# A Fourier layer, an RWKV channel mix and a Mish layer in one kernel: the first transform step with native fp32 operands for every piece

## Chip, cores and metric

The kernel runs on one core of one Trainium2 chip. The metric is the device time of one execution in microseconds, lower is better; of several runs the median is given. Every tensor is fp32 outside the kernel, and the outputs have to agree with the reference to fp32-like accuracy: this is why most operands of TensorE stand in two halves of a reduced type (fp32r), a high half `h` and a low half `l`, and most products are three matmuls (high by high, high by low, low by high).

## What is computed

With 4 sequences of 3072 rows and 256 columns, the reference is, cut to what matters:

```
X  = rfft(x, axis=1)                         # over the 3072 rows
Yr = Xr @ w_r - Xi @ w_i + b_r ; Yi = Xr @ w_i + Xi @ w_r + b_i
Y  = soft threshold of Yr and Yi by 0.01
y  = irfft(Y)                                # back to 3072 rows
xk, xr = mixes of y with y shifted by one row
r * ((relu(xk @ w_k) ** 2) @ w_v)            # r = sigmoid(xr @ w_r)
h  = that @ w_in ; out = (h * tanh(softplus(h))) @ w_out
```

## The kernel before

**The Fourier transform** is done in two steps of matmuls. Row number n is written as 32 n1 + n2, with n1 below 96 and n2 below 32. *Step one* (`s1`) multiplies, for each n2, the 96 x 256 matrix of x by a 96 x 96 matrix of cosines and sines. It goes by pieces of four n2: 8 pieces for each of the 4 sequences, 32 in all, numbered i = 8b + q. A piece is loaded into a tile `xs` (96 x 1024), its four products come into two PSUM tiles `s1p`, are copied out by `s1_ev` (two copies of 96 x 512), and are stored to DRAM. *Step two* (`s2`) reads them back in 48 units u of two groups of rows (tile `A`), 12 units for a sequence. For each unit the kernel then mixes with w_r and w_i (`mix`), adds the two parts (`yt`), applies the threshold (`above`, `shrink`, in the course of which GpSimd moves halves of the tile Y), and does the first inverse step (`is1`), whose result is stored to DRAM. The *last inverse step* (`is2`, its results copied out by `is2_ev`) belongs to the next stage, which goes by 32 tiles of 384 rows, but for the first two tiles it is done early, between the last units (`early`).

**Two forms of step one.** The first 12 pieces (`NAT = 12`) use x and the matrix as they are, in fp32: one matmul instruction of the program for each product. For the 20 others, x is split by `split_x` into `xh` (ScalarE, line 77) and `xl` (VectorE, line 78), the matrix has been split into FC by `split_F`, and each product is three matmuls (line 333).

**The order of work** is the order of the code. No scheduler moves anything: each engine has one queue, which it follows in order, and the buffers of a tile pool (`bufs=`) are reused in turn. DMAs are issued by SyncE (SP), also in order. An iteration of the transform loop, number u, issues `s2(u+1)`; the copies of `is1(u-3)`; the copies and stores of the last piece; the split of the s2 result into `Xh` (ScalarE) and `Xl` (VectorE); up to two steps of a background queue (`bg`), which loads and decodes the weights of the next stage on VectorE; a load and a split of `A`; `mix(u)`; the split of `Y(u-1)`; `above` and `shrink` of unit u; if the iteration is in `S1_AT`, a piece of step one with the load of piece i + 3 and the split of piece i + 2; `is1(u-2)`; two more background steps. The PSUM tile of `s2` has one buffer, so `s2(u+2)` on TensorE waits for `Xl` of unit u+1. Iterations 2 to 5 and two of each three from 8 to 30 hold a piece.

At the end of the loop, at u = 48 and 49, `early(14)` and `early(15)` do the last inverse step of the second tile, four products of each of its halves at a time.

The functions that the change touches and what calls them:

Of the kernel before, what the change touches and what calls it, by code (L numbers as in the profile page):

```python
# [8 lines left out]
F32 = mybir.dt.float32  # L9
F32R = mybir.dt.float32r  # L10
# [7 lines left out]
B, S, D, FK, FF = 4, 3072, 256, 1024, 2048  # L18
N1, N2 = 96, 32
NG = 12  # L20
NU = B * NG
# [8 lines left out]
def kernel(  # L30
# [27 lines left out]
    nc = tc.nc  # L58
# [13 lines left out]
    def split(src, hi, lo, lo_eng=None, hi_eng=None):  # L72

        if hi_eng is nc.vector:
            nc.vector.tensor_copy(out=hi, in_=src)
        else:
            nc.scalar.copy(out=hi, in_=src)  # L77
        (lo_eng or nc.vector).tensor_tensor(out=lo, in0=src, in1=hi, op=ALU.subtract)  # L78
# [66 lines left out]
    pkp = pk.__enter__()  # L145
# [5 lines left out]
    XS0 = [pkp.tile([128, 4, 4, D], F32, tag=w, name="XS0", bufs=1) for w in ("WK", "WV")]  # L151
# [4 lines left out]
    p1p = p1.__enter__()  # L156
    p1s = tc.tile_pool(name="p1s", bufs=1, side="left", reuse_waits="tile")
    p1sp = p1s.__enter__()
    ps1 = tc.tile_pool(name="ps1", bufs=2, space=PSUM, reuse_waits="tile")
    ps1p = ps1.__enter__()  # L160

    FC = p1sp.tile([128, N2, 2, N1], F32R, name="FC")
    MC = p1p.tile([128, 2, 2, 192], F32R, name="MC")
    WC = p1p.tile([128, 2, 2, 128], F32R, name="WC")
    WX = p1p.tile([128, 2, 3, 2, D], F32R, name="WX")
# [1 line left out]
    SEL = p1p.tile([128, 2, 128], F32R, name="SEL")  # L167
    ZV = p1p.tile([128, 2, 2, 128], F32R, name="ZV")

    Ft = {}  # L170

    def new_F(q):
        tag, n = ((("dec_v", 1), ("dec_b", 1)) + (("Cs", 2),) * 2 + (("A", 4),) * 4)[q]
        Ft[q] = p1p.tile([128, 512], F32, tag=tag, name="ctmp", bufs=n)

    def load_F(q):
        for c in (slice(0, 192), slice(192, 384)) if q == 0 else (slice(0, 384),):
            nc.sync.dma_start(out=Ft[q][0:N1, c], in_=c_f[:, q * 384 + c.start:q * 384 + c.stop])
            yield

    def split_F(q):
        v = Ft[q][0:N1, 0:384].rearrange("p (n c) -> p n c", n=4)
        split(v, FC[0:N1, 4 * q:4 * q + 4, 0, :], FC[0:N1, 4 * q:4 * q + 4, 1, :])

    cst = {}

# [90 lines left out]
    xs_t, xh_t, s1_t = {}, {}, deque()  # L277

    def new_x(b, q):
        t = xs_t[b, q] = p1sp.tile([128, 4, D], F32, tag="xs", name="xs", bufs=3) if b else XS0[q // 4][:, q % 4]  # L280

    def x_loads(b, q):
        xv = x[b].rearrange("(p n) d -> p n d", n=N2)[:, 4 * q:4 * q + 4, :]
# [6 lines left out]
        for _ in x_loads(b, q):  # L290
            pass

    def split_x(b, q):
        t = xs_t.pop((b, q))
        h = p1sp.tile([128, 4, D], F32R, tag="xh", name="xh", bufs=3)
        l = p1sp.tile([128, 4, D], F32R, tag="xl", name="xl", bufs=3)
        split(t[0:N1], h[0:N1], l[0:N1])
        xh_t[b, q] = (h, l)

    def warm(n):  # L300
        z = p1p.tile([128, 512], F32, tag="yt", name="zero", bufs=1)
        nc.vector.memset(z[:, 0:256], 0.0)
        p = ps1p.tile([128, 2, 512], F32, tag="s2", name="warm", bufs=1)
        for _ in range(n):
            nc.tensor.matmul(out=p[:, 0, 0:256], lhsT=z[:, 0:128], rhs=z[:, 0:256], start=True, stop=True)

    NAT = 12

    def s1(b, q):
        i = 8 * b + q  # L310
        plain = i < NAT
        if plain:
            h = xs_t.pop((b, q))
            f = Ft[q][:, 0:384].rearrange("p (n c) -> p n c", n=4)
        else:
            h, l = xh_t.pop((b, q))
        if b == 0:
            st = XS0[q // 4][0:N1, q % 4]
        elif i < 11:
            st = pkp.tile([N1, 4, D], F32, tag=("D", "Dh", "Dl")[q], name="st", bufs=1)  # L320
        else:
            st = p1sp.tile([N1, 4, D], F32, tag="st", name="st", bufs=2)
        for e in range(2):
            p = ps1p.tile([N1, 2, D], F32, tag=("s1" if i >= NAT or e == 0 else "mx"), name="s1p")
            for m in range(2):
                n2 = 4 * q + 2 * e + m
                if plain:
                    nc.tensor.matmul(  # L328
                        out=p[:, m, :], lhsT=f[0:N1, 2 * e + m, :], rhs=h[0:N1, 2 * e + m, :], start=True, stop=True
                    )  # L330
                    continue
                for k, (w, v) in enumerate(((0, h), (0, l), (1, h))):
                    nc.tensor.matmul(
                        out=p[:, m, :], lhsT=FC[0:N1, n2, w, :], rhs=v[0:N1, 2 * e + m, :],
                        start=(k == 0), stop=(k == 2),
                    )
            s1_t.append((b, q, e, st, p))

    def s1_ev():
        b, q, e, st, p = s1_t.popleft()  # L340
        if e == 1 or 8 * b + q >= NAT:
            nc.scalar.copy(out=st[:, 2 * e:2 * e + 2, :], in_=p)
        else:
            nc.vector.tensor_copy(out=st[:, 0:2, :], in_=p)
        if e == 1 and b == 0:
            nc.sync.dma_start(out=scr1a[:, 4 * q:4 * q + 4, :], in_=st[0:32])
            if q < 4:
                store_rest(q)
        elif e == 1 and 8 * b + q >= 11:
            nc.sync.dma_start(out=scr1[b][:, 4 * q:4 * q + 4, :], in_=st)  # L350
        elif e == 1:
            kept[q] = st
# [6 lines left out]
    def store_rest(q):  # L359
        nc.sync.dma_start(out=scr1[0][32:N1, 4 * q:4 * q + 4, :], in_=XS0[q // 4][32:N1, q % 4])  # L360
# [57 lines left out]
    def mix(u):  # L418
        hl = Xh.pop(u)
        last = u % NG == GS  # L420
        p = ps1p.tile([128, 2, D], F32, tag="mx", name="mxp")
        k1 = ps1p.tile([128, D], F32, tag="k1", name="k1p", bufs=1)

        def terms(c, w):
            return [
                (hl[a][:, dh, 128 * c:128 * c + 128], WX[:, dh, w, b, :])
                for dh in range(2) for (a, b) in ((0, 0), (0, 1), (1, 0))
            ]

        def put(out, ts, start, stop=True):  # L430
            for i, (a, w) in enumerate(ts):
                nc.tensor.matmul(out=out, lhsT=a, rhs=w, start=(start and i == 0), stop=(stop and i == len(ts) - 1))  # L432

        put(k1, terms(2, 0), True)
        nc.tensor.matmul(out=p, lhsT=SEL[:, int(last), :], rhs=BR, start=True, stop=False)
        put(p[:, 0, :], terms(1, 2), False, False)
        ts = terms(0, 1)
        if last:
            ts += [(ZV[:, a, dh, :], WX[:, dh, 0, b, :]) for dh in range(2) for (a, b) in ((0, 0), (0, 1), (1, 0))]
        put(p[:, 1, :], ts, False)  # L440
        ks = p1p.tile([128, D], F32, tag="K1", name="K1", bufs=1)
        nc.scalar.copy(out=ks, in_=k1)
        t = p1p.tile([128, 2, D], F32, tag="yt", name="yt", bufs=1)
        nc.vector.tensor_tensor(out=t, in0=p, in1=ks.unsqueeze(1).to_broadcast([128, 2, D]), op=ALU.add)  # L444
        mx_t[u] = t
# [153 lines left out]

    warm(3)  # L600
    for q in range(8):
        new_F(q)
        new_x(0, q)
    def load_both(q):
        for _ in zip(load_F(q), x_loads(0, q)):
# [3 lines left out]
        load_both(q)  # L609
    for q in range(8):  # L610
        s1(0, q)
        split_F(q)
        s1_ev()
        s1_ev()
        if q < 3:
            load_both(q + 5)
        elif q == 3:
            load_consts()
            load_x(1, 0)
        elif q == 4:  # L620
            load_x(1, 1)
# [39 lines left out]
    split_A(2)  # L661
    load_A(4)
    split_W()
    split_x(1, 4)
    split_A(3)

    WK = pkp.tile([128, 2, 2, FK], F32R, tag="WK", name="WK", bufs=1)
# [59 lines left out]
    U_E = 32  # L727
    for u in range(NU + 3):
        if 0 < u < NU - 1:
            s2(u + 1)  # L730
        if u > 2:
            is1_ev(u - 3)
        if s1_t:
            s1_ev()

        def fill():
            while s1_t:
                s1_ev()
            if u > 2:
                bg(2)  # L740

        if 0 < u < NU - 1:
            s2_ev(u + 1, fill)
        else:
            fill()
        if u + 5 < NU:
            load_A(u + 5)
        if 0 < u < NU - 3:
            split_A(u + 3)
        if u < NU:  # L750
            mix(u)
        if 1 <= u <= NU:
            split_Y(u - 1)
        if u < NU:
            above(u)
            shrink(u)
        if u == 0:
            load_x(1, 6)
            split_x(1, 5)
        if u in S1_AT:  # L760
            i = 8 + S1_AT[u]
            s1(*divmod(i, 8))
            if i + 3 < 8 * B:
                load_x(*divmod(i + 3, 8))
            if i + 2 < 8 * B:
                split_x(*divmod(i + 2, 8))
        if NU <= u < NU + 2:
            early(u - U_E - 2)
        if 2 <= u < NU + 2:
            is1(u - 2)  # L770
        if u > 2:
            bg(2)
        if u == U_E:
            p1s.__exit__(None, None, None)
            pEg = tc.tile_pool(name="pE", bufs=1, side="left", reuse_waits="tile")
            pE[0] = pEg.__enter__()
        if U_E < u < NU - 1:
            early(u - U_E - 1)
# [425 lines left out]
    for P in range(2, 8 * NBLK + LAG):  # L1204
        t, q = divmod(P, 8)
# [111 lines left out]
```

## Time and profile before

| | |
|---|---|
| median of 3 runs | 1999.83 us (1996.97 to 2003.06) |
| the profiled execution | 2000.01 us, span 1998.0 us |
| TensorE (PE) busy | 1966.9 us, 98% |
| weight loads (PEld) busy | 1867.9 us, 93% |
| VectorE (DVE) busy | 1517.6 us, 76% |
| ScalarE (ACT) busy | 1172.5 us, 59% |
| GpSimd (POOL) busy | 121.9 us, 6% |

The shares are means over three stages: the transforms (to about 320 us), the channel mix (to about 1000 us) and the Mish layer. Engine names: PE is TensorE's matmuls, PEld its weight loads, which overlap them, DVE VectorE, ACT ScalarE, POOL GpSimd, SP the queue that issues DMAs. L333 is line 333 of the kernel. Each row of a timeline has start, duration, engine, line, operation, the tiles written and read, and in brackets how long the engine had been idle and what ended that. A matmul's end is modelled and holds its way through the array, so matmuls in a row overlap; the pitch between their starts is what they cost. A native fp32 matmul of the program shows as two MATMUL records, each with its weight load.

### The profile page before, as it was taken

What the parts mean: (1) busy time and instruction counts of PE and PEld (TensorE: products, weight loads), DVE (VectorE), ACT (ScalarE), POOL (GpSimd) and SP (SyncE); (2) the same over time, 40 slices, a digit from 0 to 9 for tenths busy, and PEclk for the clock granted to TensorE, in tenths of its full rate; (3) what the DMA queues carried; (4) which work ended last, traced back from release to release, by engine and by line L of the source; (5) the groups of instructions that cost most, each with busy time, mean ns of one, the idle gap of its engine ahead of it and who ended that gap; (6) DMA issues with size and microseconds to landing.
All of it is one profiled execution on the core that took longest, in us unless ns stands there. A gap on an engine that the chain in (4) does not pass through costs nothing.

```text
span 1998.0 us, 33277 instructions
## 1 busy us (share of the span) xinstructions
PE 1966.9 (98%) x13026; PEld 1867.9 (93%) x13026; DVE 1517.6 (76%) x2441; ACT 1172.5 (59%) x1793; POOL 121.9 (6%) x196
## 2 busy tenths in 40 slices
PE   8999999999999999999999999999999999999999
PEld 6988888999999999999999999999999999999998
DVE  5889897677777777776587778777787877787785
ACT  4777777777777777776544444444444444444444
POOL 1333331000000000000000000000000000000000
PEclk9999999999999999999999999999999999999999
DMA  9666532112121121211101001001000010000000
GB/s 289 182 192 198 170 110 84 60 51 78 49 68 61 57 70 51 68 49 42 41 22 32 22 24 30 22 22 33 22 29 25 22 32 22 23 31 22 22 12 22
DMA packets 71745, 123.04 MB, mean 62 GB/s; under 512 B 6370, under 2 KB 48580, under 8 KB 71588
## 3 DMA queue, kind: packets, MB, share of 16 engines
q1 hardware_dynamic: 68004, 108.33, 18.2%
q0 software_dynamic: 3584, 12.58, 1.6%
q8 instruction: 103, 1.69, 0.4%
q14 instruction: 54, 0.44, 0.1%
HBM read 70.56 MB, written 50.33 MB: 61 GB/s over the span
## 4 chain that ended last, share of the span: by engine, by line
PE 89%; DVE 5%; ACT 3%; issue 2%; DMA 1%; POOL 0%; SPq 0%; DVEq 0%; ACTq 0%; POOLq 0%
PE h L1133 20%; PE o L1181 18%; PE kp L879 14%; PE vp L917 13%; PE o L1182 9%; PE pp L856 3%; PE p L1133 3%; PE pp L556 3%; PE s2p L389 1%; DVE Xl L78 1%; PE mxp L432 1%; PE s1p L328 1%; DVE yt L444 1%; PE hp L822 1%; ACT xh L77 1%
## 5 line engine op out<-in xcount | busy, mean ns | idle before, releaser
L1181 PE MATMUL o<-WO,gh 128*128 128x512 f32 x1536 | 562.0, 394 | 0.0
L1182 PE MATMUL o<-WO,gl 128*128 128x256 f32 x1536 | 430.3, 280 | 0.0
L1133 PE MATMUL h<-xS,WS 128*128 128x256 f32 x2208 | 350.9, 281 | 0.0
L1146 ACT COPY p1s<-p 128x256 f32<-128x256 f32 x184 | 68.5, 372 | 472.0 <-PE p L1133 471.0
L1181 PEld LDWEIGHTS o<-WO,gh 128*128 128x128 f32 x1536 | 288.9, 188 | 43.3
L1133 PEld LDWEIGHTS h<-xS,WS 128*128 128x128 f32 x2208 | 299.6, 188 | 16.1
L879 PE MATMUL kp<-xk,WK 128*128 128x384 f32 x1536 | 291.0, 337 | 0.0
L1182 PEld LDWEIGHTS o<-WO,gl 128*128 128x128 f32 x1536 | 289.5, 188 | 0.2
L917 PE MATMUL vp<-kh,WV 128*128 128x384 f32 x1024 | 281.3, 336 | 0.0
L879 PEld LDWEIGHTS kp<-xk,WK 128*128 128x128 f32 x1536 | 267.6, 189 | 0.3
L1136 DVE TENSOR_TENSOR C<-h,p1s 128x512 f32<-128x512 f32 x184 | 126.9, 690 | 157.7 <-PE h L1133 154.8
L904 DVE TENSOR_TENSOR kl<-kr,kh 128x768 fp32r<-128x768 f32 x128 | 122.8, 959 | 161.4 <-ACT kr L903 161.2
L1118 DVE TENSOR_TENSOR gl<-g,gh 128x1024 fp32r<-128x1024 f32 x184 | 223.4, 1214 | 2.1 <-ACT g L1115 2.1
L1114 ACT ACTIVATE gh<-C 128x1024 fp32r<-128x1024 f32 x184 | 195.7, 1064 | 10.6 <-DVE C L1136 10.5
L1115 ACT ACTIVATE g<-C 128x1024 f32<-128x1024 f32 x184 | 193.1, 1049 | 0.0
L1133 PE MATMUL h<-xS,WI 128*128 128x256 f32 x1104 | 189.8, 280 | 0.0
L1136 DVE TENSOR_TENSOR C<-h,wu 128x512 f32<-128x512 f32 x368 | 187.2, 550 | 0.3 <-PE h L1133 0.3
L917 PEld LDWEIGHTS vp<-kh,WV 128*128 128x128 f32 x1024 | 186.3, 188 | 0.0
L917 PE MATMUL vp<-kl,WV 128*128 128x384 f32 x512 | 171.5, 335 | 0.0
L902 ACT ACTIVATE kh<-kr 128x768 fp32r<-128x768 f32 x128 | 108.3, 846 | 89.1 <-PE vp L917 89.0
L1133 PEld LDWEIGHTS h<-xS,WI 128*128 128x128 f32 x1104 | 155.7, 188 | 0.0
L1136 DVE TENSOR_TENSOR wu<-h,C 128x512 f32<-128x512 f32 x184 | 126.4, 687 | 35.7 <-PE h L1133 31.8
(189 smaller groups left out, 3166.3 us busy)
## 6 DMA issues: line engine op xcount, KB each, us to landing
scr<-Cs SPq DMA_DIRECT2D x48, 256.0 KB
D<-scr SPq DMA_DIRECT2D x32, 384.0 KB
x2d<-r POOLq DMA_DIRECT2D x32, 384.0 KB, 3.5
x<-x2d SPq DMA_DIRECT2D x24, 512.0 KB
out_dram<-ob SPq DMA_DIRECT2D x96, 128.0 KB
A<-scr SPq DMA_DIRECT2D x44, 256.0 KB
xs<-in_x_dram SPq DMA_DIRECT2D x24, 384.0 KB
scr<-st SPq DMA_DIRECT2D x24, 384.0 KB
```

Source lines behind the costliest of these rows:

```text
L879: nc.tensor.matmul(out=p[:, m, 0:TA], lhsT=WK[:, dh, w, f * 128:(f + 1) * 128], rhs=hl[:, v, dh, :], start=(i == 0), stop=(i == 5),)
L902: nc.scalar.activation(out=kh, in_=kr, func=AF.Square)
L904: nc.vector.tensor_tensor(out=kl, in0=kr, in1=kh, op=ALU.subtract)
L917: nc.tensor.matmul(out=p[:, o, 0:TA], lhsT=WV[:, f, w, o * 128:(o + 1) * 128], rhs=v[:, m, :], start=(f == 0 and i == 0), stop=(f == 7 and ...
L1114: nc.scalar.activation(out=gh, in_=c, func=AF.Mish)
L1115: nc.scalar.activation(out=g, in_=c, func=AF.Mish)
L1118: nc.vector.tensor_tensor(out=gl, in0=g, in1=gh, op=ALU.subtract)
L1133: nc.tensor.matmul(out=out, lhsT=a(l), rhs=xS[:, v, b, :], start=(n == 0), stop=(n == 2))
L1136: nc.vector.tensor_tensor(out=out, in0=x0, in1=x1, op=ALU.add)
L1146: nc.scalar.copy(out=p1s, in_=p1)
L1181: nc.tensor.matmul(out=o[m], lhsT=gh[:, m2, ms], rhs=WO[:, f], start=(f == 0), stop=False)
L1182: nc.tensor.matmul(out=o[m][:, 0, :], lhsT=gl[:, m2, ms], rhs=WO[:, f, 0, :], start=False, stop=(f == 15))
```

## The change

All 32 pieces of step one take the native form. FC holds the unsplit fp32 matrix and is loaded directly; `split_F` and `split_x` go, and with them the tiles `xh`, `xl` and `st`. The results of a piece are copied over its own x, in `xs`, which gets seven buffers in place of three. Apart from that, in the last two iterations the early inverse steps are issued ahead of the split of Y instead of behind the pieces.

```
-    FC = p1sp.tile([128, N2, 2, N1], F32R, name="FC")
+    FC = p1sp.tile([N1, N2, N1], F32, name="FC")
...
-    def split_F(q):
-        v = Ft[q][0:N1, 0:384].rearrange("p (n c) -> p n c", n=4)
-        split(v, FC[0:N1, 4 * q:4 * q + 4, 0, :], FC[0:N1, 4 * q:4 * q + 4, 1, :])
...
-        t = xs_t[b, q] = p1sp.tile([128, 4, D], F32, tag="xs", name="xs", bufs=3) if b else XS0[q // 4][:, q % 4]
+        t = xs_t[b, q] = p1sp.tile([128, 4, D], F32, tag="xs", name="xs", bufs=7) if b else XS0[q // 4][:, q % 4]
...
-    def split_x(b, q):
-        t = xs_t.pop((b, q))
-        h = p1sp.tile([128, 4, D], F32R, tag="xh", name="xh", bufs=3)
-        l = p1sp.tile([128, 4, D], F32R, tag="xl", name="xl", bufs=3)
-        split(t[0:N1], h[0:N1], l[0:N1])
-        xh_t[b, q] = (h, l)
...
     def s1(b, q):
...
+        x_ = xs_t.pop((b, q))[0:N1]
         for e in range(2):
-            p = ps1p.tile([N1, 2, D], F32, tag=("s1" if i >= NAT or e == 0 else "mx"), name="s1p")
+            p = ps1p.tile([N1, 2, D], F32, tag=("s1" if 8 * b + q >= 12 or e == 0 else "mx"), name="s1p")
             for m in range(2):
...
-                for k, (w, v) in enumerate(((0, h), (0, l), (1, h))):
-                    nc.tensor.matmul(
-                        out=p[:, m, :], lhsT=FC[0:N1, n2, w, :], rhs=v[0:N1, 2 * e + m, :],
-                        start=(k == 0), stop=(k == 2),
-                    )
-            s1_t.append((b, q, e, st, p))
+                nc.tensor.matmul(
+                    out=p[:, m, :], lhsT=FC[:, 4 * q + 2 * e + m, :], rhs=x_[:, 2 * e + m, :], start=True, stop=True
+                )
+            s1_t.append((b, q, e, x_, p))
...
     split_W()
-    split_x(1, 4)
     split_A(3)
...
         if u < NU:
             mix(u)
+        if NU <= u < NU + 2:
+            early(u - U_E - 2)
         if 1 <= u <= NU:
             split_Y(u - 1)
...
         if u == 0:
             load_x(1, 6)
-            split_x(1, 5)
         if u in S1_AT:
             i = 8 + S1_AT[u]
             s1(*divmod(i, 8))
             if i + 3 < 8 * B:
                 load_x(*divmod(i + 3, 8))
-            if i + 2 < 8 * B:
-                split_x(*divmod(i + 2, 8))
-        if NU <= u < NU + 2:
-            early(u - U_E - 2)
         if 2 <= u < NU + 2:
             is1(u - 2)
```

On VectorE, in the middle of the transform loop, an iteration with a piece stood like this between two Xl (dec_v and dec_b are decode steps of the weights, Al, yt, Yl and Y belong to the units):

```order
L78 TENSOR_TENSOR Xl<-s2p,Xh 128x768
L78 TENSOR_TENSOR Al<-A,Ah 128x512
L444 TENSOR_TENSOR yt<-mxp,K_1165 128x512
L78 TENSOR_TENSOR Yl<-Y,Yh 128x512
L455 SCALAR_TENSOR_TENSOR Y<-yt,yc 128x512
L78 TENSOR_TENSOR xl<-xs,xh 96x1024
L118 TENSOR_SCALAR dec_v<-dec_raw 128x512
L78 TENSOR_TENSOR Xl<-s2p,Xh 128x768
```

and the same place with the change:

```order
L78 TENSOR_TENSOR Xl<-s2p,Xh 128x768
L78 TENSOR_TENSOR Al<-A,Ah 128x512
L406 TENSOR_TENSOR yt<-mxp,K_1064 128x512
L78 TENSOR_TENSOR Yl<-Y,Yh 128x512
L417 SCALAR_TENSOR_TENSOR Y<-yt,yc 128x512
L118 TENSOR_SCALAR dec_v<-dec_raw 128x512
L78 TENSOR_TENSOR Xl<-s2p,Xh 128x768
```

Only xl has gone from the queue between the two Xl; ScalarE loses the cast xh in the same way, and TensorE's twelve matmuls of line 333 become four instructions of line 296.

On ScalarE, at the end of the loop (u = 48 to 50), the rows from the last but one Yh on stood like this (yT and ya are the copies of the early inverse steps, Cs those of `is1`):

```order
L77 CAST Yh<-Y 128x512
L449 ACTIVATE yc<-yt 128x512
L486 COPY Cs<-i1p 128x512
L77 CAST Yh<-Y 128x512
L566 COPY yT<-yT 128x3x32 x2
L569 COPY ya<-s1p 128x192
L566 COPY yT<-yT 128x3x32 x2
L569 COPY ya<-s1p 128x192
L486 COPY Cs<-i1p 128x512
L569 COPY ya<-s1p 128x192 x2
L486 COPY Cs<-i1p 128x512
```

and with the change:

```order
L77 CAST Yh<-Y 128x512
L411 ACTIVATE yc<-yt 128x512
L448 COPY Cs<-i1p 128x512
L528 COPY yT<-yT 128x3x32 x2
L531 COPY ya<-s1p 128x192
L528 COPY yT<-yT 128x3x32 x2
L531 COPY ya<-s1p 128x192
L77 CAST Yh<-Y 128x512
L448 COPY Cs<-i1p 128x512
L531 COPY ya<-s1p 128x192 x2
L448 COPY Cs<-i1p 128x512
```

The last Yh has moved from ahead of the first two pairs of yT and ya to behind them; TensorE's own order there is unchanged, and SP issues the same transfers in the same order.

## Rows read from the trace of the kernel before

**Rows 1.** Windows (span, busy us of PE, PEld, DVE, ACT, POOL; clock, DMA).

```profile
15.00:20.00 5.00, 5.00 (x25) 3.76 (x24) 3.27 (x6) 2.79 (x7) 0.00 (x0) 1.00 1.05 352
35.00:40.00 5.00, 3.45 (x17) 2.88 (x18) 4.46 (x6) 2.37 (x5) 3.73 (x5) 0.79 1.03 310
51.03:230.75 179.72, 170.23 (x1286) 160.93 (x1287) 159.91 (x224) 136.32 (x257) 57.98 (x91) 0.98 0.62 185
230.75:310.76 80.01, 74.67 (x562) 69.31 (x561) 74.18 (x121) 56.13 (x112) 26.94 (x47) 1.00 0.42 127
320.00:600.00 280.00, 280.00 (x1684) 280.00 (x1683) 201.30 (x333) 206.11 (x297) 9.04 (x13) 1.00 0.21 63
```

**Rows 2.** Chain that ended last: starts of step two in undisturbed iterations.

```profile
58.70 1.32 PE s2p L389 x12
...
64.55 1.33 PE s2p L389 x12
...
173.17 1.32 PE s2p L389 x12
...
177.60 1.32 PE s2p L389 x12
```

**Rows 3.** Waits of PE from 51 to 231 us: total, times, longest.

```profile
PE s2p L389 <- DVE Xl L78: 9.6, 8, 2.2
PE s1p L333 <- ACT st L342: 1.3, 3, 0.8
```

**Rows 4.** The chain ahead of the longest wait.

```profile
154.71 1.04 ACT xh L77
...
155.77 1.36 DVE xl L78
...
158.74 0.88 DVE Xl L78
...
159.66 1.50 PE s2p L389 x10
```

**Rows 5.** Native pieces before: timeline of PE, then line 328's durations (ns, min/median/max).

```profile
19.76 1.67 PE L328 MATMUL s1p<-XS,ctmp 96*96 96x256 f32 x7
22.15 1.94 PE L328 MATMUL s1p<-XS,ctmp 96*96 96x256 f32 x8 [0.71 <-DMA XS<-in_x_dram]
...
38.06 3.48 PE L328 MATMUL s1p<-xs,ctmp 96*96 96x256 f32 x8
...
L328 PE MATMUL s1p<-XS,ctmp x64: 379/379/713, 3.9 to 23.7; 96*96 96x256 f32 x64
```

**Rows 6.** Groups by line, 51.03 to 230.75 us: the splits of x.

```profile
L78 DVE TENSOR_TENSOR xl<-xs,xh 96x1024 fp32r<-96x1024 f32 x18 | 24.4, 1358 | 4.4 <-ACT xh L77 4.4
L77 ACT CAST xh<-xs 96x1024 fp32r<-96x1024 f32 x18 | 18.6, 1033 | 0.0
```

**Rows 7.** Timeline of ACT, DVE and PE at the loop's start.

```profile
47.69 1.03 ACT L77 CAST xh<-xs 96x1024 fp32r<-96x1024 f32 x1
...
48.75 1.36 DVE L78 TENSOR_TENSOR xl<-xs,xh 96x1024 fp32r<-96x1024 f32 x1 [0.25 <-ACT xh L77]
50.04 0.94 DVE L78 TENSOR_TENSOR Xl<-s2p,Xh 128x768 fp32r<-128x768 f32 x1
...
51.03 0.47 PE L389 MATMUL s2p<-MC,Ah 128*128 128x192 f32 x2 [2.13 <-DVE Xl L78]
```

**Rows 8.** Timeline of ACT, DVE and PE at the loop's end.

```profile
314.91 0.62 ACT L77 CAST Yh<-Y 128x512 fp32r<-128x512 f32 x1 [1.80 <-POOL Y L459]
...
315.56 0.69 DVE L78 TENSOR_TENSOR Yl<-Y,Yh 128x512 fp32r<-128x512 f32 x1 [2.12 <-ACT Yh L77]
...
316.79 0.33 PE L556 MATMUL s1p<-ifh,Dh 96*128 96x192 f32 x1 [2.66 <-ACT ya L569]
```

**Rows 9.** Chain that ended last: the first matmuls of the next stage, later ones.

```profile
319.39 5.03 PE kp L879 x24
...
326.50 2.08 PE kp L879 x12
```

More of the change, by code (lines that the diff above doesn't have):

```diff
@@ L168 @@
     ZV = p1p.tile([128, 2, 2, 128], F32R, name="ZV")
[L170 to L174, printed above, removed]
     def load_F(q):
+        v = FC[:, 4 * q:4 * q + 4, :].rearrange("p n c -> p (n c)")
         for c in (slice(0, 192), slice(192, 384)) if q == 0 else (slice(0, 384),):
-            nc.sync.dma_start(out=Ft[q][0:N1, c], in_=c_f[:, q * 384 + c.start:q * 384 + c.stop])
+            nc.sync.dma_start(out=v[:, c], in_=c_f[:, q * 384 + c.start:q * 384 + c.stop])
             yield
-    def split_F(q):
-        v = Ft[q][0:N1, 0:384].rearrange("p (n c) -> p n c", n=4)
-        split(v, FC[0:N1, 4 * q:4 * q + 4, 0, :], FC[0:N1, 4 * q:4 * q + 4, 1, :])
     cst = {}
@@ L305, in warm @@
             nc.tensor.matmul(out=p[:, 0, 0:256], lhsT=z[:, 0:128], rhs=z[:, 0:256], start=True, stop=True)
-    NAT = 12
     def s1(b, q):
[L310 to L322, printed above, removed]
+        x_ = xs_t.pop((b, q))[0:N1]
         for e in range(2):
-            p = ps1p.tile([N1, 2, D], F32, tag=("s1" if i >= NAT or e == 0 else "mx"), name="s1p")
+            p = ps1p.tile([N1, 2, D], F32, tag=("s1" if 8 * b + q >= 12 or e == 0 else "mx"), name="s1p")
             for m in range(2):
-                n2 = 4 * q + 2 * e + m
-                if plain:
-                    nc.tensor.matmul(
-                        out=p[:, m, :], lhsT=f[0:N1, 2 * e + m, :], rhs=h[0:N1, 2 * e + m, :], start=True, stop=True
-                    )
-                    continue
-                for k, (w, v) in enumerate(((0, h), (0, l), (1, h))):
-                    nc.tensor.matmul(
-                        out=p[:, m, :], lhsT=FC[0:N1, n2, w, :], rhs=v[0:N1, 2 * e + m, :],
-                        start=(k == 0), stop=(k == 2),
-                    )
-            s1_t.append((b, q, e, st, p))
+                nc.tensor.matmul(
+                    out=p[:, m, :], lhsT=FC[:, 4 * q + 2 * e + m, :], rhs=x_[:, 2 * e + m, :], start=True, stop=True
+                )
+            s1_t.append((b, q, e, x_, p))
     def s1_ev():
         b, q, e, st, p = s1_t.popleft()
-        if e == 1 or 8 * b + q >= NAT:
+        if e == 1 or 8 * b + q >= 12:
             nc.scalar.copy(out=st[:, 2 * e:2 * e + 2, :], in_=p)
@@ L601 @@
     for q in range(8):
-        new_F(q)
         new_x(0, q)
@@ L611 @@
         s1(0, q)
-        split_F(q)
         s1_ev()
```

## Prediction

> **What bounds the kernel now.** I read the page first, for where TensorE waits at all: over the whole span it is 98% busy. A table of windows then splits the span at three iteration starts of the transform loop [rows 1]. From 320 us on TensorE has no idle time: whatever the transforms save there arrives undiminished at the end, and nothing later can give more. In the opening the DMA engines are full (share 1.05 in 15 to 20 us) and TensorE has work all the same. What is left is the loop, in two parts: the 30 iterations u = 2 to 31 (51.03 to 230.75 us, 179.72 us), twenty of which hold a piece of step one, and those behind (80.01 us), which hold none.
>
> What an undisturbed iteration takes is read from the chain that ended last, where it runs through TensorE alone [rows 2]. From the s2 at 58.70 to the next at 64.55 is 5.85 us with a piece in it, from 173.17 to 177.60 is 4.43 us without; the difference, 1.42, is the piece's twelve matmuls. So the 30 iterations need 20 x 5.85 + 10 x 4.43 = 161.3 us, and 2.1 more for three that have six additional ZV matmuls of the same 256 columns: 163.4. They take 179.7. **16.3 us are lost there.**
>
> Who takes them: TensorE's waits in this stretch [rows 3] are 9.6 us for Xl, VectorE's low half of the s2 result (2.13 of it is the wait that ends at 51.03, counted below, so 7.5 inside, in seven waits), and 1.3 for copies on ScalarE. The granted clock of the stretch is 0.98 of 2.4 GHz; the missing 0.02, time at 1.2 GHz, is another 3.6 us. The last 4 us I cannot name. The longest wait shows the mechanism [rows 4]: ScalarE casts the x piece (xh, 1.04 us), VectorE subtracts (xl, 1.36), two decode steps of the weights follow in its queue, then Xl, and only then does TensorE get its s2 at 159.66, after 2.21 us of idling. VectorE is busy 159.91 of 179.72 us and in order, so a late xl makes Xl late.
>
> **The change, part by part.**
>
> *Splits of x.* They go: in the loop 18 of the 20 stand in the stretch, 24.4 us on VectorE and 18.6 on ScalarE [rows 6]; the two before it are priced under the opening. VectorE's load falls to 159.9 - 24.4 = 135.5 us. In each chain like that of rows 4, 1.36 us leaves VectorE, and the wait for xh ahead of it. The seven waits are 1.1 us each on the average, less than that; the longest is 2.21, and the stretch has two pieces to every iteration without one, so that a second xl is seldom far ahead. So I take the Xl waits in this stretch as gone, and with them the clock loss and the unnamed part, which I put down to them; the copies' waits stay. Remaining: 1.5 of the 16.3 us. Bounds: all 16.3 go, or half (8.2) stay, because the weights' decode steps are still in VectorE's queue ahead of an Xl (two of them fill the time from xl's end at 157.13 to 158.74 in rows 4).
>
> *Native products.* Four products of a piece cost 12 matmuls now. The native form is already in the trace, in the first twelve pieces [rows 5]: each product leaves two matmul rows of 379 ns, and an undisturbed piece lasts 1.94 us for eight of them, drain of the last included. Start to start that is (1.94 - 0.38) / 7 = 0.223 us, so 8 x 0.223 = 1.78 us, against 1.42: 0.37 us more per piece with the fractions kept, 7.4 us for twenty. Their weight loads overlap, as they do in those rows. The lower end is the other undisturbed row, seven in 1.67 us, a pitch of 0.215 and 6 us; the upper end is the row at 38.06, in a stretch with a granted clock of 0.79 [rows 1]: 3.48 us, 2.06 more, 41 us in all. I take 7.4, since the loop's clock is high.
>
> The Trainium skill, FP8 and Floating Point Precision, section TensorE Precision Notes, says that true fp32 takes four passes through the array; three split products would thus become four, 1.42 x 4/3 = 1.89 us a piece, 9.5 us for twenty, and the whole sum 2 us smaller than mine. By that rule, the trace agrees: two records for a product, 0.223 us each, are nearly four of the split form's 1.42 / 12 = 0.118.
>
> *The loop thus gains* 16.3 - 1.5 - 7.4 = **7.4 us** (ends: 0.7, with half the losses kept; 10.3, with all gone and the lower price).
>
> *Opening.* Eight splits of FC go from ScalarE and VectorE; while they ran TensorE had work from the DMAs, so nothing; without that cover, by the xh row and 384 columns for 1024, an estimated 0.4 us a piece. Two x splits stood between 43 and 50 us: the row at 51.03 waits 2.13 us for an Xl behind an xl of 1.36, which had waited for an xh of 1.03 [rows 7]. ScalarE's cast of that s2 stood behind the xh too. Without both, Xl is ready about 2.4 us earlier, when TensorE comes to it: **2.1 us** (ends 1.3 and 2.3).
>
> *Seven buffers, results over x.* The SP queue has the same transfers in the same order; a load reuses a buffer whose store was issued four pieces before. TensorE has no wait for x in the loop, so nothing; a late load would stop a piece, and, behind it on SP, the loads of A. A ScalarE copy overwrites only what the matmuls that it waits for have read.
>
> *Last inverse steps ahead of the last split.* At u = 48 ScalarE's last Yh waits for GpSimd until 314.91, and the copies ya, for which TensorE waits 2.66 us, stand behind it in order [rows 8]. It had idled 1.80 us until then. Ahead of it, ScalarE does the copies from 313.1 on, while GpSimd still moves Y; what now lies between Yh's start and TensorE's step is 1.88 us, 0.62 of it Yh, so that step starts near 314.4 instead of 316.79. What is late next is the last inverse step itself: Yl, 315.56 to 316.25, is not moved, so its three matmuls of 512 columns (like six of a piece's, 0.7 us) run from 316.25 to about 316.95 and the next stage starts there, not at 319.39: 2.4 us. The 24 kp matmuls at its head take 5.03 us, partly at the low clock, against twice 2.08 where it is high [rows 9]. If TensorE does not idle long enough for the clock to fall, 0.9 more. I take **3.0** (ends 2.0 and 3.3; Yh would wait only if the copies ahead of it outlasted GpSimd).
>
> *The 80.01 us between* lose no work and gain none: 0.
>
> **Sum.** 7.4 + 2.1 + 3.0 = 12.5 us. The profiled execution took 2000.01 us with a span of 1998.0, its median over three runs is 1999.83, the same to 0.01%. 2000.0 - 12.5 = **1987.5 us**.
>
> **Rivals.**
> - *The waits stay.* VectorE's decode steps and ScalarE's order fill the place of xl. For it: VectorE is 93% busy in the iterations without any x split [rows 1], which still idle. Against it: there its extra work is the moved inverse steps. Half the losses stay, the tail gives its lower end: 0.7 + 2.1 + 2.0 = 4.8, 1995.2 us.
> - *All goes.* Loop 10.3, opening 2.3, tail 3.3: 15.9, 1984.1 us.
> - *Slower: native pieces run in the loop as in the row at 38.06.* Place: the twenty pieces; price 41 us, less the 19.9 gained elsewhere (14.8 + 2.1 + 3.0): 2021 us. It decides from 1.00 us more per piece, 2.42 in all; by 0.3% slower from 2.72. For it: that row is a native piece. Against it: it lies among waits for DMA, and the uninterrupted pieces are at 2.4 GHz.
> - *Hidden.* Step two turns out to wait for what step one stores, or the stage at 319 for a load: no gain, near 1999 us. Against it: TensorE shows no DMA wait in the loop.
>
> **Chances.** Forecast (1985.5 to 1990.5) 0.50, all goes 0.12, waits stay (1990.5 to 1997) 0.23, hidden 0.07, slower 0.08. A measurement of this kernel can tell about 0.3%, 6 us. Below 1994 lies the first two and somewhat under half of the third: faster 0.72, same 0.20, slower 0.08. The range leaves out the slower and the hidden case and the edges: 1983.5 to 1996.5; the likeliest one's own is 1985.5 to 1990.5.
>
> **What would show it.** Right: MATMUL rows of the pieces 379 ns, eight in 1.7 to 1.8 us; iterations of 6.2 and 4.43 us; TensorE's wait for Xl between 51 and 231 us (now 9.6) under 2; the loop's 30 iterations near 172.3 us; the first kp near 307.5, its 24 near 4.2 us. Wrong: Xl waits of 4 us or more there; a piece over 2 us; a wait of TensorE for xs; a wait of 2 us before the last i1p.

## The result and the profile after

The changed kernel took **1983.52 us** (median of 4 runs, 1983.27 to 1984.00) against 1999.97 (1996.97 to 2003.06) for the kernel before on the same chip: a ratio of 0.9918, 95% interval 0.9901 to 0.9935. That is 16.4 us faster, 4.0 below the predicted 1987.5, outside the forecast's own 1985.5 to 1990.5, and inside the stated range (1983.5 to 1996.5) by 0.02 us. By the medians it is the case "all goes" (1984.1) that came.

The page of the changed kernel: the span, TensorE's busy share, and the share of the engines in the chain that ended last.

```profile
span 1981.8 us, 33049 instructions
PE 1962.0 (99%) x12946; PEld 1861.4 (94%) x12946; DVE 1486.5 (75%) x2413; ACT 1154.0 (58%) x1765; POOL 106.7 (5%) x196
...
PE 95%; DVE 2%; DMA 1%; ACT 1%; issue 0%; POOL 0%; SPq 0%; DVEq 0%; ACTq 0%; POOLq 0%
```

The table of windows: the 30 iterations u = 2 to 31, twenty of them with a piece, then iterations 32 to 45, then the tail (from the last s2 to the first kp).

```profile
46.81:216.23 169.42, 169.42 (x1207) 156.53 (x1206) 134.82 (x207) 122.50 (x241) 43.56 (x91) 1.00 0.67 201
216.23:288.97 72.74, 68.75 (x510) 64.12 (x508) 68.17 (x113) 51.01 (x103) 24.74 (x42) 0.98 0.44 135
288.97:302.63 13.66, 12.27 (x80) 10.82 (x79) 10.65 (x25) 9.56 (x23) 4.30 (x9) 0.94 0.21 73
```

In the first row TensorE is busy for the whole of its 169.42 us, at a clock of 1.00. The same 30 iterations took 179.55 us before, cut at the first matmul of their s2 (the 179.72 of [rows 1] end 0.17 later); they are down by 10.1. The list of TensorE's waits for this stretch, before 9.6 us for Xl (2.13 of it the wait that ends where the stretch begins) and 1.3 for copies [rows 3], is empty. The chain that ended last runs through TensorE alone:

```profile
53.24 1.32 PE s2p L351 x12
...
56.97 1.73 PE s1p L296 x8
58.70 0.69 PE i1p L436 x3
59.38 0.65 PE s2p L351 x6
```

From s2 to s2 (53.24 to 59.38) an iteration with a piece takes 6.14 us, where 6.2 was predicted; its eight native records (L296) last 1.73. The tail, in the same view:

```profile
296.60 0.62 ACT Yh L77
...
298.22 0.35 ACT yT L528 x2
...
299.45 1.24 PE s1p L518 x8
...
300.72 0.42 ACT Cs L448
...
301.18 1.65 PE i1p L436 x3
302.83 4.96 PE kp L835 x24
```

The copies of the early inverse steps now follow the last Yh but one, and the last Yh is no longer in the chain. TensorE's wait for ya, 2.66 us before [rows 8], is 0.2. What is late next is a copy on ScalarE (Cs), which stands behind the last Yh: the last inverse step starts when that copy is done, before VectorE has finished the last Yl.

```profile
300.68 0.69 DVE L78 TENSOR_TENSOR Yl<-Y,Yh 128x512 fp32r<-128x512 f32 x1 [0.82 <-ACT Yh L77]
```

```profile
301.18 0.80 PE L436 MATMUL i1p<-Yh,WC 128*128 128x512 f32 x1 [0.51 <-ACT Cs L448]
```

The next stage starts 16.6 us earlier than before [rows 9]. Its 24 kp take 4.96 us, about as long as before: in this execution TensorE's granted clock was 0.59 from 300.63 to 302.63 us and 0.56 in the two us behind, where the kp begin. In the nine other kernels below that have the move the 24 kp take 4.16 to 4.19 us.

### The profile page after: what moved, and what is told of

It is laid out like the page before. It is cut to its first block, busy times and chain, and to the rows that moved or that the text cites. A ratio compares the mean times of both kernels' runs of the same rounds, so it can differ in the third digit from the quotient of the medians.

```text
span 1981.8 us, 33049 instructions
## 1 busy us (share of the span) xinstructions
PE 1962.0 (99%) x12946; PEld 1861.4 (94%) x12946; DVE 1486.5 (75%) x2413; ACT 1154.0 (58%) x1765; POOL 106.7 (5%) x196
## 4 chain that ended last, share of the span: by engine, by line
PE 95%; DVE 2%; DMA 1%; ACT 1%; issue 0%; POOL 0%; SPq 0%; DVEq 0%; ACTq 0%; POOLq 0%
PE h L1089 20%; PE o L1137 18%; PE kp L835 14%; PE vp L873 13%; PE o L1138 9%; PE pp L812 3%; PE p L1089 3%; PE mxp L394 3%; PE pp L518 3%; PE s2p L351 2%; PE s1p L296 2%; PE k1p L394 1%; PE i1p L436 1%; PE hp L778 1%; DMA XS<-in_x_dram 1%
```

## Experiments

The stretches below are cut in every kernel's profile, one execution each, as above: the *opening* ends with the s2 that begins iteration 2, the *loop* is the 30 iterations behind it, *behind the loop* means iterations 32 to 45, the *tail* ends with the first kp, and the rest is the remainder of the span. The unit is us; "before" is split at its own s2(3), s2(33) and s2(47), so its loop is 179.55.

| kernel | opening | loop | behind the loop | tail | rest | span |
|---|---|---|---|---|---|---|
| before | 51.03 | 179.55 | 73.28 | 15.33 | 1678.82 | 1998.0 |
| changed | 46.81 | 169.42 | 72.74 | 13.66 | 1679.22 | 1981.8 |
| splits of x kept | 51.49 | 181.60 | 72.77 | 13.02 | 1678.27 | 1997.1 |
| cast alone | 50.01 | 174.28 | 72.69 | 13.03 | 1678.29 | 1988.3 |
| subtract alone | 50.27 | 172.87 | 72.66 | 13.02 | 1678.38 | 1987.2 |
| three matmuls, no splits | 49.49 | 163.59 | 72.73 | 13.03 | 1678.28 | 1977.1 |
| tail as before | 49.39 | 169.42 | 72.72 | 16.08 | 1679.50 | 1987.1 |
| early move alone | 51.35 | 180.95 | 74.34 | 13.04 | 1677.91 | 1997.6 |
| splits of FC kept | 48.35 | 169.61 | 72.77 | 13.05 | 1678.32 | 1982.1 |
| three buffers | 49.16 | 169.28 | 72.72 | 13.03 | 1678.28 | 1982.5 |
| bias loads early | 48.90 | 169.37 | 72.66 | 13.02 | 1678.32 | 1982.3 |
| decode later | 48.68 | 169.56 | 73.35 | 13.02 | 1678.37 | 1983.0 |

**The splits of x kept, as idle work.** The native products stay; xh and xl are computed at their old places and nobody reads them.

```
+    def split_x(b, q):
+        t = xs_t[b, q]
...
+        split(t[0:N1], h[0:N1], l[0:N1])
...
+            if i + 2 < 8 * B:
+                split_x(*divmod(i + 2, 8))
```

> The changed kernel, with the two splits of x kept as idle work: ScalarE casts xh and VectorE subtracts xl at their old places in the queues, and nobody reads them. TensorE keeps the native products. Theory (the gain came out of ScalarE's and VectorE's queues): the waits for Xl come back, now behind a dearer TensorE, and the loop's 30 iterations take 178 us or more instead of 169.4; 1994 to 2003 us against 1983.5. Rival (the buffers, the earlier transfers or the native form itself made the gain): under 1987 us, the iterations at 170.

Measured: 1998.39 us (1995.91 to 1999.87), ratio 0.9988, interval 0.9979 to 0.9997. Nearly all of the gain is gone. The loop's windows, and TensorE's waits in it (us in total, times, longest):

```profile
51.49:233.09 181.60, 175.01 (x1204) 158.87 (x1205) 160.41 (x225) 136.73 (x258) 58.15 (x90) 0.98 0.63 186
```

```profile
PE s2p L357 <- DVE Xl L78: 8.0, 7, 2.1
PE s1p L302 <- ACT xs L310: 0.6, 1, 0.6
```

Of the 8.0 us, 2.1 are the wait that ends where the loop begins; the other six waits, 5.9 us, stand at iterations that had one before (there seven, 7.5 us). The clock of 0.98 and the loop's length are back too. The longest wait inside, 1.6 us, has the chain of before [rows 4] again:

```profile
156.04 1.04 ACT xh L77
157.10 1.36 DVE xl L78
158.46 0.81 DVE dec_b L128
159.30 0.77 DVE dec_v L132
160.07 0.88 DVE Xl L78
...
160.99 1.86 PE s2p L357 x12
```

So the loop's gain comes from the splits that are gone, not from the form of the matmuls or the buffers.

**One half of each split kept.** In one kernel ScalarE's cast xh alone, in the other a subtract of the same shape on VectorE (x minus itself, so that it waits for no cast), both idle work at the old places.

```
+        nc.scalar.copy(out=h[0:N1], in_=xs_t[b, q][0:N1])
```

```
+        nc.vector.tensor_tensor(out=l[0:N1], in0=t, in1=t, op=ALU.subtract)
```

> The changed kernel with ScalarE's casts of x alone kept as idle work, 1.03 us for each of 20 pieces, and no subtraction on VectorE. Theory (VectorE's load is what made Xl late; ScalarE has room, 58% busy): under 1985.5 us. Rival (the chain went through the cast on ScalarE as well, whose queue holds the cast Xh): 1988 us or more.

> The changed kernel with VectorE's subtractions alone kept as idle work (x minus x, 1.36 us for each of 20 pieces), and no cast on ScalarE. Theory (VectorE's load is what made Xl late): most of the loss comes back, 1990 us or more, with waits for Xl of 4 us or more between 47 and 216 us. Rival (without the wait for the cast, VectorE has room: 135.5 + 27 = 162.5 of 169 us): under 1986 us.

Measured: with the cast alone 1990.26 us (1989.75 to 1993.36), ratio 0.9956, 0.9941 to 0.9971; with the subtract alone 1988.10 (1986.44 to 1989.90), 0.9941, 0.9924 to 0.9957. The cast alone is what its rival expected (1988 or more); the subtract alone lies between its theory and its rival. Waits from the loop's start, cast first, then subtract:

```profile
PE s2p L355 <- DVE Xl L78: 3.0, 6, 1.3
PE s1p L300 <- ACT xs L308: 0.5, 2, 0.2
```

```profile
PE s2p L356 <- DVE Xl L78: 3.1, 2, 2.3
```

The longest wait of each list, 1.3 and 2.3 us, is again the one that ends where the loop begins; inside, TensorE waits for Xl five times with the cast (1.7 us in all) and once with the subtract (0.75). Against the changed kernel's loop the cast costs 4.9 us, the subtract 3.5, and both as a chain 12.2, which is 3.9 more than the sum; by the medians of the runs, with the opening in them, the three cost 6.7, 4.6 and 14.9 us, 3.6 more than the sum. Neither engine's load alone makes the stall. The cast delays Xh behind it on ScalarE, as in this chain, where Xh starts at 134.92:

```profile
132.93 1.03 ACT xh L286
...
135.65 0.97 DVE Xl L78
136.67 1.58 PE s2p L355 x12
```

The subtract delays Xl on VectorE: ahead of the wait of 0.75 us the chain is xl at 151.37, two decode steps, Xl at 154.11 and the s2 at 155.03. The subtract that waits for its cast does both in a row.

A part of these costs is clock. With the subtract alone iteration 2 takes 7.78 us, against 6.28 in the changed kernel, at a granted clock of 0.78, right behind the wait of 2.3 us that ends the opening: 1.5 of its 3.5 us. Before, it was the same: of the time at the low clock that the loop lost, nearly all stands in iteration 2 (7.51 us at a clock of 0.77, undisturbed 5.85), behind the opening's wait of 2.13 us, and in iteration 20 (7.50 us at 0.77), behind the longest wait.

**Three matmuls without splits.** The products of the last 20 pieces are three fp32r matmuls again, on two tiles written once ahead of the loop; so pieces 12 to 31 use neither x nor their own matrix, and TensorE has the work of before without the splits.

```
...
+                for k in range(3):
+                    nc.tensor.matmul(out=p[:, m, :], lhsT=FR, rhs=XR, start=(k == 0), stop=(k == 2))
```

> The price of the native form by itself: in pieces 12 to 31 each product is three fp32r matmuls again, but on two constant fp32r tiles made once from FC, so that no split is needed; these pieces do not use x or their part of the matrix, everything else is as in the changed kernel. Theory (TensorE now sets the pace of every iteration with a piece, and the native form costs 6.14 - 5.85 = 0.29 us a piece more): 5.8 us less, 1977.7 us, iterations of 5.85 us. Rival (part of the price is covered, since VectorE or ScalarE are as late): 1980 to 1983.5 us, with waits for Xl in the stretch. Rival by the first price of the prediction (0.37): 1976.1.

Measured: 1979.56 us (1978.16 to 1981.69), ratio 0.9900, 0.9885 to 0.9915. Its loop, and a piece of it in the chain that ended last:

```profile
49.49:213.08 163.59, 163.59 (x1286) 158.47 (x1285) 134.33 (x207) 120.78 (x241) 43.96 (x91) 1.00 0.71 209
```

```profile
65.21 1.43 PE s1p L303 x12
```

This measures both sides of the loop's sum, in the profiled executions. TensorE's work of before takes 163.59 us undisturbed, so the stalls of before cost 179.55 - 163.59 = 15.96 us (the prediction had 16.3). The native form costs 169.42 - 163.59 = 5.83 us for twenty pieces, 0.29 each (predicted 0.37). By the medians this kernel is only 4.0 us faster than the changed one, 1.9 slower than expected, and just below the rival that covers part of the price; but that rival's sign, waits for Xl in the stretch, is absent here. The profiled execution, 1978.89, is the second fastest of the four; what the slower ones lose, and where, their times don't tell.

**The tail as before.** The early inverse steps stand behind the pieces again, all else is as in the changed kernel.

```
-        if NU <= u < NU + 2:
-            early(u - U_E - 2)
         if 1 <= u <= NU:
             split_Y(u - 1)
...
+        if NU <= u < NU + 2:
+            early(u - U_E - 2)
         if 2 <= u < NU + 2:
             is1(u - 2)
```

> The changed kernel with the early inverse steps at u = 48 and 49 back behind the split of Y. Theory (the move is worth what the stretch from the last s2 to the first kp lost, 15.33 to 13.67 us): 1.7 us more, 1985.2, and a wait of TensorE for ya of over 2 us again. Rival (without the x splits ScalarE is early enough anyway): within 0.5 us of 1983.5.

Measured: 1988.96 us (1987.80 to 1989.98), ratio 0.9940, 0.9923 to 0.9957; the kernel with three buffers, below, took 1983.71 on the same chip. The wait for ya is back, as expected, but the loss is 5.25 us and not the expected 1.7, which was worked out from the changed kernel's own tail, 13.67 us and partly at the low clock. Its longest wait in the tail, the chain that ended last there, and windows of 2 us:

```profile
PE s1p L518 <- ACT ya L531: 2.7, 1, 2.7
```

```profile
302.60 0.62 ACT Yh L77
303.21 0.35 ACT yT L528 x2
...
307.81 5.26 PE kp L835 x24
```

```profile
301.60:303.60 2.00, 0.19 (x1) 0.00 (x0) 0.35 (x1) 1.00 (x4) 0.84 (x3) 0.90 0.39 131
303.60:305.60 2.00, 1.12 (x5) 1.15 (x6) 1.22 (x7) 1.23 (x5) 0.00 (x0) 0.50 0.00 0
305.60:307.60 2.00, 2.00 (x8) 1.72 (x7) 1.15 (x7) 0.64 (x2) 0.00 (x0) 0.50 0.39 131
307.60:309.60 2.00, 2.00 (x8) 1.99 (x7) 0.98 (x2) 1.76 (x3) 0.00 (x0) 0.50 0.12 41
```

TensorE is busy for 0.19 of 2 us while it waits for ScalarE's last Yh, and then works at a granted clock of 0.50, which is 1.2 GHz, through the last inverse steps and the first kp, to 309.60. With the move the clock does not fall in the same place of the kernel with three buffers (windows, then the chain):

```profile
299.00:301.00 2.00, 1.33 (x10) 1.11 (x9) 1.30 (x3) 2.00 (x7) 0.13 (x1) 1.00 0.00 0
301.00:303.00 2.00, 1.65 (x10) 1.04 (x8) 1.09 (x7) 1.32 (x5) 1.07 (x3) 1.00 0.39 131
```

```profile
303.38 0.97 PE i1p L443 x3
304.35 4.18 PE kp L842 x24
```

The 24 kp take 4.18 us, against 5.26 without the move and 5.03 before [rows 9]. The move's gain is thus part wait, part clock: by the two profiles 16.08 - 13.03 = 3.05 us in the tail, 1.22 in the rest.

**The early move alone**, in the kernel before.

```
+        if NU <= u < NU + 2:
+            early(u - U_E - 2)
         if 1 <= u <= NU:
             split_Y(u - 1)
...
-        if NU <= u < NU + 2:
-            early(u - U_E - 2)
         if 2 <= u < NU + 2:
             is1(u - 2)
```

> The kernel before, with the early inverse steps of the last two iterations ahead of the split of Y, and all else (the splits of x and FC, three buffers) as it was. Theory: the move's gain does not hang on the rest: 3.0 us by the forecast, up to 5 by the run without the move; 1995 to 1997, with the first kp near 315 to 316 and its 24 near 4.3 us. Rival: the move pays only where the loop ahead of it is free of stalls: 1999 to 2000.

Measured: 1996.28 us (1994.02 to 1999.73), before 1999.43 (1997.48 to 2002.83) on the same chip: ratio 0.9985, 0.9976 to 0.9994. The gain of 3.15 us does not hang on the rest of the change. Tail and rest are 3.2 us shorter than before's, and the kp at full clock:

```profile
318.87 0.97 PE i1p L474 x3
319.84 4.16 PE kp L879 x24
```

The first kp of this execution stood at 319.84, not at 315 to 316 as expected: the loop of this execution took 1.4 us more than before's and the iterations behind 1.1 more.

**The splits of FC kept, and three buffers.** Two parts that the prediction costs at nothing: in one kernel the eight splits of FC are done as idle work into a tile that nobody reads, in the other xs has three buffers and the results go to the tiles `st` of before.

```
+        split_F(q)
         s1_ev()
```

```
-        t = xs_t[b, q] = p1sp.tile([128, 4, D], F32, tag="xs", name="xs", bufs=7) if b else XS0[q // 4][:, q % 4]
+        t = xs_t[b, q] = p1sp.tile([128, 4, D], F32, tag="xs", name="xs", bufs=3) if b else XS0[q // 4][:, q % 4]
...
+            st = p1sp.tile([N1, 4, D], F32, tag="st", name="st", bufs=2)
...
-            s1_t.append((b, q, e, x_, p))
+            s1_t.append((b, q, e, st, p))
```

> The changed kernel with the eight splits of FC kept as idle work at their old places in the opening. Theory now (the 1.9 us by which the opening gained more than was forecast came from these, through the stores and loads that stand behind the copies on SP): 1985 to 1986 us, and the first product of bias and SEL starts near 43 us, not 41.3. Rival, as in the prediction (they cost nothing, the DMA engines set the opening, and the 1.9 us is a matter of one execution): 1983.5 within 0.5 us.

> The changed kernel with xs in three buffers again and the results of step one in tiles of their own, as before. Theory, as in the prediction (seven buffers and results over x are worth nothing in time): 1983.5 within 0.5 us. Rival (the opening's loads start earlier because of the seven buffers): 1985 us or more, the first product of bias and SEL near 43 us.

Measured: 1984.66 us (1983.86 to 1985.40), ratio 0.9919, 0.9904 to 0.9933, and 1983.71 (1982.17 to 1984.24), 0.9913, 0.9898 to 0.9927. The buffers give nothing that can be measured. The FC splits cost at most about 1 us, the difference of the two medians, whose ranges overlap. Their expectation's sign, the first product of bias and SEL near 43 us, came (42.86), but the other native kernels, without these splits, have it at 41.3 to 44.0, so it says nothing about them.

**Bias loads early.** The opening's first matmul with BR waits for that tile (1.3 us, "PE mxp <- POOL BR" in the changed kernel); here the loads of the biases are issued ahead of x(1, 0).

```
+            load_bias()
             load_x(1, 0)
...
     load_consts()
-    load_bias()
```

> A version that might beat both: the changed kernel with the two 1 KB loads of the bias issued ahead of the second sequence's first x load in place of behind the constants. The chain of the changed kernel runs through that load, GpSimd's copies and BR into the first mix, for which TensorE waits 1.3 us. Theory: the mix starts up to 1.4 us earlier, 1982.1 us. Rival (the x load or s2 behind it is late next): 1983.5 within 0.3 us.

Measured: 1984.13 us (1983.22 to 1984.57), ratio 0.9922, 0.9907 to 0.9936: no gain. The wait for BR is gone, yet the matmul that had it starts at 42.75 us, later than the changed kernel's 41.31. TensorE's waits for x up to 48.90 us:

```profile
PE s1p L296 <- DMA xs<-in_x_dram: 2.2, 1, 2.2
PE s1p L296 <- DMA XS<-in_x_dram: 1.9, 2, 1.8
```

These 4.1 us are no more than the changed kernel's 5.1; but the granted clock from 35 to 40 us was 0.54 in this execution and 0.68 in the changed kernel's. What sets the opening's length is left open here.

**Decode later.** The longest wait for Xl that the changed kernel still has behind the opening, 1.82 us, ends ahead of the s2 that begins iteration 36 (the expectation counts it as 35), behind this queue of VectorE (timeline of the changed kernel):

```profile
232.31 0.69 DVE L128 SCALAR_TENSOR_TENSOR dec_b<-dec_raw,dec_b 128x512 f32<-128x512 uint32 x1
233.03 0.77 DVE L132 TENSOR_TENSOR dec_v<-dec_v,dec_b 128x512 f32<-128x512 f32 x1
233.72 0.61 DVE L78 TENSOR_TENSOR Dpl<-Dp,Dph 96x256 fp32r<-96x256 f32 x1
234.26 0.74 DVE L78 TENSOR_TENSOR ifh<-ift,ifh 96x384 fp32r<-96x384 f32 x1
234.93 0.94 DVE L78 TENSOR_TENSOR Xl<-s2p,Xh 128x768 fp32r<-128x768 f32 x1
```

```
-        if u > 2:
+        if u > 2 and u not in (U_E + 2, U_E + 3):
             bg(2)
```

> The changed kernel, with the two background steps at the end of u = 34 and u = 35 left for later iterations, where VectorE idles from u = 41 on. In the profiled executions of the native kernels the one long wait of TensorE for Xl that is left (1.82 us, at the start of iteration 35) and a shorter one behind it (0.75 us) stand behind a queue on VectorE that holds two decode steps (0.68 and 0.77 us) beside the splits Dpl and ifh. Theory: the order on VectorE alone makes these waits; without the two steps the first wait falls by about 1.4 us and the second goes, with some time at the low clock: 2 to 3 us, 1980.5 to 1981.5. Rival: VectorE is full from u = 33 to 40, so the steps that were put off make a later Xl late by as much: 1983.5, no difference.

Measured: 1984.75 us (1983.71 to 1987.29), ratio 0.9927, 0.9915 to 0.9940: no gain over the changed kernel. The waits from 215 to 320 us, first of this kernel, then of the one with three buffers:

```profile
PE s2p L351 <- DVE Xl L78: 4.0, 7, 1.6
```

```profile
PE s2p L358 <- DVE Xl L78: 4.7, 7, 1.8
```

The wait in question fell to 0.48 us as the theory had it, but one of 1.6 us stands seven iterations later, where the kernel with three buffers has 0.79: VectorE's last decode step (WR, 0.69 us), put off to that place, stands in the queue ahead of that Xl. The rival holds: VectorE is nearly full there (68.17 of 72.74 us in the changed kernel), and what leaves one iteration is late in another. None of these runs found a kernel that is faster than the changed one and computes the same.

## Why the prediction was right, and where it was off

- *What bounds the kernel: right.* The undisturbed loop was worked out at 163.4 us and measured at 163.59. The losses, 16.3 predicted, are 15.96. Some 1.7 of them, iteration 2 at the low clock, belong to the opening's wait and not to those of the loop.
- *Splits of x: the mechanism right, one term too careful.* With the splits back the stalls are back, in the same iterations. The residual of 1.5 us (the copies' waits stay) was wrong: it measured 0. Those waits hung on the cast in ScalarE's queue as well: waits for copies come back with the cast alone (0.5 us), not with the subtract alone.
- *Native products: the mechanism right, the price mis-sized.* 5.83 us for twenty instead of 7.4. I had taken the pitch from the row with 1.94 us, which begins behind a wait of 0.71 us (its first pitch is 0.265, the others are 0.216), when the row without a wait [rows 5] gave 0.215. In the loop eight records take 1.73 us, a pitch of 0.216. The Trainium skill, FP8 and Floating Point Precision, section TensorE Precision Notes, counts four passes for true fp32. By that rule, the trace agrees: 1.73 us at 2.4 GHz are 4152 cycles for 4 products of 256 columns, 4.05 passes each if a pass is a cycle per column. The extra cost is below the third that the prediction worked out from the rule because the split form stands above its three passes: 1.43 us are 3432 cycles, 3.35 passes.
- *The loop's gain* therefore was 179.55 - 169.42 = 10.1 us, not 7.4; these two terms are most of the miss, 2.7 of about 4 us.
- *Opening: right.* 2.1 us predicted. The wait of 2.13 us for Xl ahead of s2(3) is in none of the seven kernels without any split of x; with both splits kept it is 2.14, with the subtract alone 2.31, with the cast alone 1.30. These seven (changed, three matmuls, tail as before, FC splits, three buffers, bias, decode) reach s2(3) at 46.81 to 49.49, median 48.90, against 51.03: 2.1. The changed kernel's own 46.81 is the earliest of them; "tail as before" and "decode later" are the same program up to iteration 34 and stand at 49.39 and 48.68, so that about 2 us of its profiled span are an early execution and no effect. Its late clock at the tail (1.6 us in tail and rest against the three-buffer kernel) nearly cancels them. The kernels that keep some of the splits of x stand at 50.01 to 51.49.
- *FC splits and seven buffers at nothing: right*, within about 1 us.
- *The early move: the gain right, one wait misnamed.* 3.0 predicted; alone it gave 3.15, and undoing it in the changed kernel cost 1988.96 - 1983.71 = 5.25 by the medians, 4.3 by tail and rest of the profiles. Both parts were in the sum: the wait went, and where the clock holds the kp take 4.2 us, as forecast. The last inverse step, though, was to wait for VectorE's Yl and waits for ScalarE's Cs; that the time comes out alike (from the start of the last Yh to the first kp 2.1 us in the three-buffer kernel, 2.04 in the forecast) is luck. Of the 2 us that the move is worth more in the changed kernel, the profiles show half: there, without it, the clock stands at 0.50 from 303.60 to 309.60 us, where before it was 1.00 until 317.19, then 0.64 and 0.51 for two us each. The other half stays open.
- *The iterations behind the loop at 0: nearly.* 73.28 became 72.7 in most of the kernels, 0.5 us, and the rival *waits stay* is right about this stretch alone: in the kernel with three buffers TensorE still waits 4.7 us for Xl there.
- *The rivals.* "All goes" came, for its own reason: the lower price and no residual. "Waits stay", "hidden" and "slower" fell; no native piece in the loop was slow (the 160 matmul rows take 377 to 381 ns). The price of "slower" was too high in any case: 3.48 us is the row at 38.06 with the drain of its last matmul, which the 1.78 leave out; from its start to the next matmul, at 41.12, it is 3.06.
- *The range: luck.* The forecast had 0.50 and "all goes" 0.12. Two cautious terms in the loop, both wrong to the same side, carried the time to the range's end, which held by 0.02 us.

By stretches of the three-buffer kernel against before: 1.87 + 10.27 + 0.56 + 2.30 + 0.54 = 15.5 us, its span's difference (1998.0 - 1982.5).

## What to carry to other kernels

Where the engine that bounds a kernel stalls behind another engine's chain, compute what it needs undisturbed from iterations without a stall; here the whole difference was the prize of removing the chain. A more expensive instruction on that engine can pay if it removes work from a serial chain of two others. Breaking the chain at either link gave back more than half of it here: of the 12.2 us that cast and subtract cost together, 7.3 without the subtract and 8.7 without the cast. Take a price from a row in an uninterrupted stretch rather than from one that begins with a wait.

## What the runs showed of the hardware

- A product of 96 x 96 by 96 x 256 costs 4.05 cycles of 2.4 GHz per column as a native fp32 matmul, which shows as two records with a pitch of 0.216 us, and 3.35 as three fp32r matmuls; so the native form costs 21% more (1.73 against 1.43 us a piece).
- The runs of the changed kernel scatter by 0.7 us, those of before by 6; but three matmuls without splits, whose loop has no stall, scatters by 3.5, so that the scatter doesn't go by the loop's stalls alone.
- The opening differs by over 2 us between executions of what is the same program up to the end of the transform loop: the first BR matmul starts at 41.31 us in the changed kernel's profile and at 42.29 with the tail as before, and s2(3) at 46.81 and 49.39. The DMA engines' share from 40 to 45 us is 0.98 and 1.02.
- At the tail the clock fell in one profile and held in another of almost the same program: 24 kp took 4.96 us in the changed kernel's and 4.17 in that with the biases loaded early, which differs from it in the opening alone.
